# One decode step of attention beside an MLP: wo in four pieces, b1 added by matmuls, heads spread by VectorE

## The chip, the cores and the metric

One NeuronCore of a Trainium2 chip runs the kernel. Its engines are TensorE (PE, with its weight loads as PEld), VectorE (DVE), ScalarE (ACT), GpSimd (POOL) and SyncE (SP), each with an instruction stream of its own; they meet at semaphores. Sixteen DMA engines move data between device memory and the on-chip memory (SBUF). The metric is the device time of one execution in microseconds; lower is better.

## The reference

One token of width 1024 goes through a layer norm. Branch A is attention with 32 query heads over 4 key and value heads, on the last 4096 positions of a cache; branch B is a second layer norm and an MLP of width 3584 with biases b1 and b2. Both are added to the input. All inputs are bf16.

```python
def reference(A_x, A_k_cache, A_v_cache, A_wq, A_wo, B_x, B_w1, B_b1, B_w2, B_b2):
    def _A_ref(x, k_cache, v_cache, wq, wo):
        B, Sq, D = x.shape                      # 1, 1, 1024
        Hq, Dh = 32, 128
        Hkv, Sk = k_cache.shape[1], k_cache.shape[2]   # 4, 65536
        W = min(4096, max(256, Sk // 4))        # 4096
        rep = Hq // Hkv
        q = (lambda x, *d: x.transpose(*d))((x @ wq).reshape(B, Sq, Hq, Dh), 0, 2, 1, 3)
        k = jnp.repeat(k_cache[:, :, Sk - W:, :], rep, axis=1)
        v = jnp.repeat(v_cache[:, :, Sk - W:, :], rep, axis=1)
        scores = jnp.einsum("bhqd,bhkd->bhqk", q, k) * (Dh ** -0.5)
        p = _softmax(scores, axis=-1)
        o = jnp.einsum("bhqk,bhkd->bhqd", p, v)
        return (lambda x, *d: x.transpose(*d))(o, 0, 2, 1, 3).reshape(B, Sq, Hq * Dh) @ wo

    def _B_ref(x, w1, b1, w2, b2):
        y = _layernorm(x, axis=-1)
        h = _gelu(jnp.einsum("bsd,df->bsf", y, w1) + b1)   # 3584 wide
        return jnp.einsum("bsf,fd->bsd", h, w2) + b2

    x = A_x
    xn = _layernorm(x, axis=-1)
    return x + _A_ref(xn, A_k_cache, A_v_cache, A_wq, A_wo) + _B_ref(xn, B_w1, B_b1, B_w2, B_b2)
```

## The kernel before

There is one token, so every matrix is read once and used for one row: about 40 MB come in, 8 MB each for wq and wo, 7 MB each for w1 and w2, and 4 MB each for the keys and the values that are used.

The order is written out by hand, engine by engine. SP issues all large loads on its one queue: the first half of wq, the keys of heads 0 and 1, the second half of wq, the keys of heads 2 and 3, and w1 at once (L234 to L238). Then it waits until DVE has turned the last keys (L311), issues the values over the keys' place and w2 over wq's, waits for the last matmul on w1 (L316) and issues wo in the pieces of WO_CHUNKS (L318 to L321). A piece of n rows gives every one of the 128 partitions n x 2 KB in one run. wo's first 20 rows (TAIL) lie in BIG, the last 12 in KT. ACT issues three small loads on another queue: x, b2, and b1 as 128 runs of 28 values (L170 to L172).

PE's stream, from L423 on, has these stages:

- x is copied to all partitions by two matmuls into banks 0 and 1 (L426); DVE and ACT compute the layer norms from there (L259 to L276). The matmuls of `edge` (L429) set banks 7, 0 and 1 to zero in all rows that matter, with a column HOT that has a single one.
- q: a loop over the two halves of wq, eight matmuls per turn (L443 to L451), into bank 7. Its result is turned by DVE (L293) and copied into the block pattern QBD, five blocks by DVE, three by ACT (L300 to L307). DVE turns keys before and after this (`turn_k`, L283).
- the scores (L459 to L467), in banks 3 to 6, opened by four matmuls with the mask OTHER; DVE takes the maximum (L334), ACT the exponential (L346), DVE turns the result (L350).
- EDGE (L470): two matmuls put x + b2 into bank 7, in which the output is gathered.
- h = y @ w1 in bank 0 (L485 to L488). H8 is its copy, L494 turns it to 128 partitions, DVE adds b1 (L356) and computes the gelu (L361 to L375) into GO, the row of weights of the last loop.
- pv, the values, in bank 1 (L500 to L503); DVE divides and selects (L383) and gathers the heads in ON (L389).
- the last loop, written with branches: `pe_round` (L518) takes four rows of w2 or wo per turn, eight matmuls. After TURN = 4 rounds `pe_turn_o` (L510) breaks in once: four matmuls with E4 spread ON over 128 partitions, and ACT copies the result into GO and OT (L393, L394). 12 rounds in all: 7 for w2, 5 for the first 20 rows of wo.
- the tail, unrolled (L533 to L544): the last 12 rows of wo in pieces of 9, 2 and 1, each row as four small matmuls side by side in four column groups of the array. Then DVE and ACT copy the row out of bank 7 (L397 to L401) and SP stores it.

POOL fills the constants (L177 to L225) and then turns landings into steps of one semaphore, `s_feed`, for which the loops wait (L406 to L421). So a loop's wait is on POOL's step, the tail's waits are on the landings themselves.

Of the kernel before, what the change touches and what calls it, by code (L numbers as in the profile page):

```python
# [9 lines left out]
D = 1024  # L10
# [13 lines left out]
WO_CHUNKS = [8, 12, 9, 2, 1]  # L24
WO_HEAD = 2
# [4 lines left out]
TAIL = 20  # L30
# [5 lines left out]
ROUNDS = 12  # L36
TURN = 4
# [15 lines left out]
def bass_parallel_sum__sliding_block_cached__mixer_channel_mlp__decode_kernel(  # L53
# [19 lines left out]
    def sems(name, n):  # L73
# [13 lines left out]
        "x", "h", "hT", "q", "sc", "pv", "tot", "o2", "fin")}  # L87
    s_feed = nc.alloc_semaphore("S_FEED")

    def sb(name, shape, d):  # L90
        return nc.alloc_sbuf_tensor(name, shape, d)
# [12 lines left out]
    HOT = sb("HOT", [1, 8 + 128], bf16)  # L104
    EDGE = sb("EDGE", [2, 132], bf16)
    XBRP = sb("XBRP", [2, 16 * XP], bf16)
    B1T = sb("B1T", [128, FC], bf16)
# [22 lines left out]
    ON = sb("ON", [32, DH], bf16)  # L130
# [12 lines left out]
    def bank(n, rows=128, first=0):  # L143
        return PS[first:first + rows, n * 512:(n + 1) * 512]
# [6 lines left out]
    def wo_home(row):  # L151
        return (BIG, (FC + row) * D) if row < TAIL else (KT, (row - TAIL) * D)
# [19 lines left out]
    act.dma_start(B1T[:, :], B_b1.rearrange("(p c) -> p c", c=FC)).then_inc(s_b1, 16)  # L172

    def pool_wait():
        pool.wait_ge(POOL.sem, POOL.cnt)
# [3 lines left out]
    POOL.mark(pool.memset(identb[:, :], 0.0))  # L179
    pool_wait()  # L180
# [5 lines left out]
    POOL.mark(pool.memset(HOT[:, :], 0.0))  # L186
    pool_wait()
    C["hot"] = POOL.mark(pool.memset(HOT[:, 7:8], 1.0))
# [3 lines left out]
    POOL.mark(pool.memset(QBD[:, :], 0.0))  # L192
# [33 lines left out]


# [12 lines left out]
    def dve_wait():  # L240
        dve.wait_ge(DVE.sem, DVE.cnt)
# [17 lines left out]
    layernorm_stats(PS[:, 0:1024], 0, "ln1")  # L259
    DVE.mark(dve.tensor_scalar(out=XN[:, :], in0=PS[:, 0:1024], scalar1=MV[:, 0:1], scalar2=SD[:, 0:1],  # L260
# [35 lines left out]
    dve.wait_ge(POOL.sem, C["consts"])  # L296
# [3 lines left out]
    for b in range(4):  # L300
        for c in range(PAIRS):
            to = QD[32 * b:32 * b + 32, c, :, b, 16 * c:16 * c + 16].rearrange("p e (u j) -> p e u j", j=4)
            of = QS[32 * b:32 * b + 32, :, 4 * c:4 * c + 4, :]
            if PAIRS * b + c < 5:
                C["d_QBD"] = DVE.mark(dve.tensor_copy(to, of))  # L305
            else:
                C["a_QBD"] = ACT.mark(act.activation(out=to, in_=of, func=ACTF.Copy))  # L307
# [10 lines left out]
    for j, n in enumerate(WO_CHUNKS):  # L318
        home, first = wo_home(c0)
        sp.dma_start(home[:, first:first + n * D], wo_flat[:, c0 * D:(c0 + n) * D]).then_inc(s_wo[j], 16)  # L320
        c0 += n  # L321

    def spread(first, n):
        return GO[:, LEAD + first * STEP:LEAD + (first + n) * STEP].rearrange(
            "p (r c y) -> p r c y", c=2, y=COPY)[:, :, :, 0:2 * ROUND:2]

    def rows_of(values):
        n = values.shape[1] // ROUND
        return values.rearrange("p (r u) -> p r u", u=ROUND).unsqueeze(2).to_broadcast([128, n, 2, ROUND])
# [12 lines left out]
    for b in range(4):  # L342
# [12 lines left out]
    dve.wait_ge(s_b1, 16)  # L355
    DVE.mark(dve.tensor_tensor(  # L356
        out=HT[:, :].rearrange("p (t c) -> p c t", c=4),
        in0=PS[:, 2 * 512 + 32:2 * 512 + 64].rearrange("p (c t) -> p c t", c=4)[:, :, 0:7],
        in1=B1T[:, :].rearrange("p (t c) -> p c t", c=4), op=ALU.add))
# [18 lines left out]
    DVE.mark(dve.reciprocal(out=REC[:, :], in_=PS[0:64, 2 * 512 + 64:2 * 512 + 65]))  # L378
# [9 lines left out]
    with nc.allow_low_precision(reason="one of the four terms is not zero"):  # L388
        C["on"] = DVE.mark(dve.tensor_reduce(  # L389
            out=ON[:, :], in_=ONM.rearrange("p (g d) -> p d g", g=4), axis=AX.X, op=ALU.add))  # L390
    act.wait_ge(done["o2"], 1)
    o2 = PS[:, 2 * 512:2 * 512 + 32]
    ACT.mark(act.activation(out=spread(FC // ROUND, TAIL // ROUND), in_=rows_of(o2[:, 0:TAIL]), func=ACTF.Copy))  # L393
    C["OT"] = ACT.mark(act.activation(  # L394
        out=OT[:, LEAD:LEAD + 2 * (32 - TAIL):2], in_=o2[:, TAIL:32], func=ACTF.Copy))
# [9 lines left out]

    pool.wait_ge(s_wq[0], 16)  # L406
# [13 lines left out]
    pool.wait_ge(s_wo[WO_HEAD], 16)  # L420
    pool.sem_inc(s_feed, 1)  # L421

    pe.wait_ge(POOL.sem, C["ones"])  # L423
    pe.wait_ge(s_x, 16)
    for i in range(2):
        last = pe.matmul(bank(i), lhsT=onesb[0:1, :], rhs=XB[0:1, 8 * i:8 * i + 8, :])  # L426
    last.then_inc(done["x"], 1)

    def edge(n):  # L429
        pe.matmul(bank(n), lhsT=HOT[:, 8:136], rhs=XB[0:1, 0:8, :], start=True, stop=False, skip_group_check=True)  # L430

    def add(to, lhsT, rhs, **place):
        return pe.matmul(to, lhsT=lhsT, rhs=rhs, start=False, stop=False, skip_group_check=True, **place)  # L433

    turn = pe.alloc_register("turn")
    pe.reg_mov(turn, 1)
    pe.wait_ge(POOL.sem, C["hot"])
    edge(7)
    pe.wait_ge(DVE.sem, C["xz"])
    edge(0)  # L440
    edge(1)
    pe.wait_ge(POOL.sem, C["consts"])
# [9 lines left out]

    pe.wait_ge(ACT.sem, C["q32"])
    for n in range(4):
        pe.matmul(bank(3 + n), lhsT=OTHER[:, :], rhs=ALT[:, :], start=True, stop=False, skip_group_check=True)
    pe.wait_ge(DVE.sem, C["d_QBD"])
    pe.wait_ge(ACT.sem, C["a_QBD"])
    K4 = KT[:, :].rearrange("p (x k) -> p x k", k=128)
    with pe.Fori(0, PAIRS) as c:  # L459
        pe.wait_ge(s_feed, turn)  # L460
        pe.reg_add(turn, turn, 1)
        with pe.Fori(0, 2) as j:
            for n in range(4):
                for u in range(2):
                    last = add(bank(3 + n), QBD[:, bass.ds(c * 512 + j * 256 + u * 128, 128)],
                               K4[:, bass.ds(c * 64 + 16 * n, 16), bass.ds(j * 64 + 32 * u, 32)])
                last.then_inc(done["sc"], 1)  # L467

    pe.wait_ge(s_b2, 16)
    for a in range(2):  # L470
        pe.matmul(bank(7), lhsT=EDGE[:, 1 - a:129 - a], rhs=XB[:, 8 * a:8 * a + 8, :], start=(a == 0), stop=False,
                  skip_group_check=True)
        if a == 0:
            pe.wait_ge(DVE.sem, C["mx"] - 1)

# [3 lines left out]
    first_turn = 1 + len(WQ_CHUNKS) + PAIRS  # L479
    vec, column, limit = (pe.alloc_register(n) for n in ("vec", "column", "limit"))  # L480
    PEO = [pe.engine]
    for register, value in ((vec, 0), (column, 0), (limit, first_turn + TURN)):
        pe.reg_mov(register, value)
# [7 lines left out]
    pe.matmul(PS[0:64, 2 * 512 + 64:2 * 512 + 65], lhsT=B64[:, :], rhs=SUMP[:, :]).then_inc(done["tot"], 1)  # L491
    pe.wait_ge(ACT.sem, C["a_h8"])
    for c in range(4):
        last = pe.matmul(PS[:, 2 * 512 + 32 + 8 * c:2 * 512 + 40 + 8 * c], lhsT=H8[:, c:512:4], rhs=FLIP[:, :])  # L494
# [3 lines left out]
    pe.wait_ge(s_v, 32)  # L498
    V3 = V.rearrange("p (c x) -> p c x", c=PAIRS)
    with pe.Fori(0, 8) as i:  # L500
# [5 lines left out]
    at = type(pe.snap(turn)).of_register_unchecked  # L506
    vec_at, column_at = at(vec, min_val=0, max_val=STEP * (ROUNDS - 1)), at(
        column, min_val=0, max_val=(ROUNDS - 1) * ROUND * D)
    nc.br("pe_round", engines=PEO)
    with nc.body("pe_turn_o", valid_engines=PEO):  # L510
        pe.wait_ge(DVE.sem, C["on"])
        for j in range(4):
            last = pe.matmul(PS[:, 2 * 512:2 * 512 + 32], lhsT=E4[:, j * 128:(j + 1) * 128],
                             rhs=ON[:, j * 32:(j + 1) * 32], start=(j == 0), stop=(j == 3))
        last.then_inc(done["o2"], 1)
        pe.reg_mov(limit, first_turn + ROUNDS)
        nc.br("pe_round", engines=PEO)
    with nc.body("pe_round", valid_engines=PEO):  # L518
        pe.wait_ge(s_feed, turn)
        pe.reg_add(turn, turn, 1)  # L520
        for u in range(ROUND):
            for a in range(2):
                add(bank(7), GO[:, bass.ds(vec_at + (LEAD + 2 * u - ROW - a), 128)],
                    BIG[:, bass.ds(column_at + (u * D + a * 512), 512)])
        pe.reg_add(vec, vec, STEP)
        pe.reg_add(column, column, ROUND * D)
        pe.br_lt(turn, limit, on_true="pe_round", on_false="pe_phase")
    with nc.body("pe_phase", valid_engines=PEO):
        pe.wait_ge(s_feed, turn)
        pe.br_lt(turn, first_turn + ROUNDS, on_true="pe_turn_o", on_false="pe_tail")  # L530
    nc.switch_bb("pe_tail")

    c0 = TAIL  # L533
    for j, n in enumerate(WO_CHUNKS[WO_HEAD:]):
        pe.wait_ge(s_wo[WO_HEAD + j], 16)
        for c in range(c0, c0 + n):
            home, column = wo_home(c)
            rhs = home[:, column:column + D]
            for a in range(4):
                first, column = LEAD + 2 * (c - TAIL) - (0 if a % 2 else ROW), 7 * 512 + a // 2 * 256  # L540
                last = add(PS[32 * a:32 * a + 32, column:column + 256], OT[:, first:first + 32],
                           rhs[:, TAIL_AT[a]:TAIL_AT[a] + 256], tile_position=(0, 32 * a))
        c0 += n
# [31 lines left out]
```

## Time and profile before

| what | value |
|---|---|
| time, median of 3 runs | 99.2 us (99.13 to 99.36) |
| profiled execution, time | 99.2 us |
| its span | 97.55 us |
| bytes read | 39.86 MB, 409 GB/s over the span |
| TensorE clock granted | 1.0 |
| busy: PE, PEld, DVE, ACT, POOL | 73%, 31%, 39%, 8%, 10% of the span |
| last landing of w1, of w2, of wo | 49.33, 76.01, 95.48 us |
| wo issued | 62.16 us |

The span is what the hardware profiler saw of the core; the time is a little longer, since it holds what lies around it. Every time in the text counts from the start of the span. In a row of the timeline the columns are the start, the duration, the engine, the line, the operation, what it writes and reads, and how many of them were joined; the bracket at the end is the idle time ahead of it and what ended it. A row of the DMA queues has the packets, the megabytes and the packets' time as a share of 16 engines in the stretch shown. "Packet records" are the single DMA packets behind these rows, each with its queue, start, duration and size.

### The profile page before, as it was taken

The numbers are of one execution on the slowest core, as the hardware profiler recorded it, in microseconds if no ns is written. First come the engines' busy times: TensorE is split into PE (matmuls) and PEld (weight loads), VectorE is DVE, ScalarE is ACT, GpSimd is POOL, SyncE is SP. The second block draws the span as 40 slices with busy tenths as digits, with TensorE's granted clock in tenths as the row PEclk, the third lists the DMA queues.
The fourth block names the chain that finished last, engine by engine and source line by source line (L and its number), as shares of the span: only waits on it lengthen the run. The fifth ranks groups of instructions, "written<-read, shape, count | busy, mean of one in ns | idle before, by whom it ended". The sixth has DMA issues, their size and how long they took to land.

```text
span 97.6 us, 1259 instructions
## 1 busy us (share of the span) xinstructions
PE 71.6 (73%) x337; PEld 30.1 (31%) x349; DVE 37.9 (39%) x50; ACT 8.1 (8%) x16; POOL 10.2 (10%) x29
## 2 busy tenths in 40 slices
PE   0005000399999973879979999799989999997991
PEld 0001000033444320323334444333344444443450
DVE  0001899899930699950581800050043000000001
ACT  0500000600000023000008000200000010000001
POOL 6999600000000000000000000000000000000000
PEclk9999999999999999999999999999999999999999
DMA  7599999999999998888999999999899998999980
GB/s 215 228 431 444 410 432 437 430 430 443 417 430 464 682 400 376 376 376 376 430 437 430 437 497 443 443 430 400 373 464 423 430 480 363 453 436 416 438 329 1
DMA packets 2229, 39.88 MB, mean 409 GB/s; under 512 B 434, under 2 KB 436, under 8 KB 692
## 3 DMA queue, kind: packets, MB, share of 16 engines
q1 hardware_dynamic: 2020, 39.85, 95.7%
q10 hardware_dynamic: 208, 0.01, 0.1%
q8 instruction: 1, 0.02, 0.1%
HBM read 39.86 MB, written 0.00 MB: 409 GB/s over the span
## 4 chain that ended last, share of the span: by engine, by line
DMA 79%; PE 13%; SPq 4%; issue 1%; DVE 0%
DMA BIG<-in_B_w_dram 47%; DMA KT<-in_A_wo_dram 32%; PE PS L433 13%; SPq L320 2%; SPq L232 1%; SPq L159 1%; DVE Pb L400 0%
## 5 line engine op out<-in xcount | busy, mean ns | idle before, releaser
L433 PE MATMUL PS<-BIG,GO 128*128 x84 | 20.1, 379 | 1.4 <-POOLq L419 0.5
L285 DVE STREAM_TRANSPOSE KT<-KV 128x4096 bf16<-128x4096 bf16 x4 | 17.6, 4432 | 4.8 <-DMA KV<-in_A_k_cache_dram 4.8
L433 PE MATMUL PS<-BIG,XZ 128*128 x64 | 16.2, 418 | 0.0
L433 PEld LDWEIGHTS PS<-BIG,GO 128*128 x96 | 9.3, 98 | 11.8 <-issue 1.7
L433 PE MATMUL PS<-BIG,YZ 128*128 x56 | 12.4, 380 | 0.7 <-DMA BIG<-in_B_w_dram 0.7
L433 PE MATMUL PS<-KT,QBD 128*128 x32 | 8.0, 379 | 2.6 <-DVE QBD L305 1.8
L433 PEld LDWEIGHTS PS<-BIG,XZ 128*128 x64 | 6.7, 105 | 9.9 <-issue 4.5
L400 DVE CAST Pb<-PS 64x256 bf16<-64x256 f32 x1 | 0.4, 417 | 21.7 <-PE PS L433 21.7
L433 PE MATMUL PS<-KV,KT 128*128 x32 | 8.3, 381 | 0.6
L430 PE MATMUL PS<-XBRP,HOT 1*128 1x512 bf16 x3 | 1.7, 620 | 9.0 <-DVE XZ L275 9.0
L433 PEld LDWEIGHTS PS<-BIG,YZ 128*128 x56 | 5.4, 96 | 7.5 <-issue 1.9
L426 PE MATMUL PS<-XBRP,onesb 1*128 1x512 bf16 x2 | 1.0, 605 | 8.2 <-DMA XBRP<-in_A_x_dram 8.2
L433 PEld LDWEIGHTS PS<-KT,QBD 128*128 x32 | 3.1, 96 | 7.5 <-issue 5.4
L245 DVE BATCH_NORM_STATS2 BN<-PS 128x6 f32<-128x512 f32 x2 | 1.3, 689 | 9.3 <-PE PS L426 9.3
L433 PEld LDWEIGHTS PS<-KV,KT 128*128 x32 | 3.1, 96 | 5.4 <-issue 3.9
L334 DVE TENSOR_REDUCE MX<-PS 128x1 f32<-128x1024 f32 x2 | 2.4, 1220 | 4.4 <-PE PS L433 4.4
L383 DVE SCALAR_TENSOR_TENSOR QBD<-PS,REC,HALF 32x256 f32<-32x256 f32 x2 | 0.9, 473 | 7.0 <-PE PS L433 6.9
L430 PEld LDWEIGHTS PS<-XBRP,HOT 1*128 1x128 bf16 x3 | 0.3, 118 | 10.2 <-DVE XZ L275 9.9
L350 DVE STREAM_TRANSPOSE KT<-Pb 128x2048 bf16<-128x2048 bf16 x1 | 2.3, 2312 | 2.1 <-ACT Pb L346 2.1
L356 DVE TENSOR_TENSOR HT<-PS,B1T 128x28 f32<-128x28 f32 x1 | 0.2, 209 | 7.4 <-PE PS L494 7.4
L346 ACT ACTIVATE Pb<-PS,NMB 128x2048 bf16<-128x2048 f32 x1 | 2.0, 1967 | 13.0 <-DVE NMB L343 13.0
L426 PEld LDWEIGHTS PS<-XBRP,onesb 1*128 1x128 bf16 x2 | 0.1, 98 | 8.2 <-issue 8.2
(76 smaller groups left out, 37.6 us busy)
## 6 DMA issues: line engine op xcount, KB each, us to landing
BIG<-in_A_wq_dram SPq DMA_DIRECT2D x2, 4096.0 KB, 18.9
BIG<-in_B_w_dram SPq DMA_DIRECT2D x1, 7168.0 KB, 46.0
KV<-in_A_k_cache_dram SPq DMA_DIRECT2D x2, 2048.0 KB, 23.2
KV<-in_A_v_cache_dram SPq DMA_DIRECT2D x2, 2048.0 KB, 13.4
BIG<-in_B_w_dram SPq DMA_DIRECT2D x1, 4096.0 KB, 24.6
BIG<-in_B_w_dram SPq DMA_DIRECT2D x1, 3072.0 KB, 31.2
BIG<-in_A_wo_dram SPq DMA_DIRECT2D x1, 3072.0 KB, 25.6
KT<-in_A_wo_dram SPq DMA_DIRECT2D x1, 2304.0 KB, 30.6
```

The costliest lines, as they stand in the source:

```text
L159: sp.dma_start(dst[:, c0 * width:(c0 + n) * width].rearrange("p (c n) -> p c n", c=n), src[:, c0:c0 + n, :],).then_inc(semaphores[j], 16)
L232: sp.dma_start(KV[:, c * 8192:(c + 1) * 8192], pairs(A_k_cache, c)).then_inc(s_k[c], 16)
L245: DVE.mark(dve.bn_stats(out=BN[:, 12 * n + 6 * i:12 * n + 6 * i + 6], in_=src[:, 512 * i:512 * i + 512]))
L285: C["kt", n] = DVE.mark(dve.transpose(KT[:, n * 4096:(n + 1) * 4096], KV[:, n * 4096:(n + 1) * 4096]))
L320: sp.dma_start(home[:, first:first + n * D], wo_flat[:, c0 * D:(c0 + n) * D]).then_inc(s_wo[j], 16)
L334: C["mx"] = DVE.mark(dve.tensor_reduce(out=MX2[:, n:n + 1], in_=S[:, 1024 * n:1024 * n + 1024], axis=AX.X, op=ALU.max))
L346: C["exp"] = ACT.mark(act.activation(out=Pb[:, :], in_=S, func=ACTF.Exp, bias=NMB[:, 0:1], scale=SCALE, accum_out=SUMP[:, 0:1]))
L350: C["d_pt"] = DVE.mark(dve.transpose(PT[:, 0:2048], Pb[:, :]))
L383: DVE.mark(dve.scalar_tensor_tensor(out=ONM.rearrange("p (i c d) -> p i c d", i=2, c=PAIRS)[:, i], in0=PS[rows, 512:1024].rearrange("p (c ...
L426: last = pe.matmul(bank(i), lhsT=onesb[0:1, :], rhs=XB[0:1, 8 * i:8 * i + 8, :])
L430: pe.matmul(bank(n), lhsT=HOT[:, 8:136], rhs=XB[0:1, 0:8, :], start=True, stop=False, skip_group_check=True)
L433: return pe.matmul(to, lhsT=lhsT, rhs=rhs, start=False, stop=False, skip_group_check=True, **place)
```

## The change

- wo comes in pieces of 16, 11, 4 and 1 rows instead of 8, 12, 9, 2 and 1, all into BIG. The last loop takes the first 16 rows (11 rounds in all), the unrolled tail the last 16. POOL's last step now follows the first piece of wo.
- b1 comes as 32 runs of 112 values. Four matmuls with E4, placed after the q loop, put it into the place in bank 2 (`turned`) on which the turned h is then added; DVE copies the sum instead of adding b1. The wait for the values stands among the matmuls that turn h.
- DVE spreads the heads: ON is turned as float32, then in four pieces into O2. The four matmuls on ON and the break in the last loop go, and this loop becomes a plain counted one.
- The banks are opened by ACT, which copies zeros from QBD into banks 0, 1 and 7; the three `edge` matmuls and HOT go. x is copied into banks 2 and 3. POOL zeroes QBD earlier, and steps `s_feed` only after its constants are done.
- EDGE's two matmuls move from after the scores to before them; of the eight blocks of QBD DVE copies four, ACT four, and PE's wait for ACT's part moves into the loop.

The changed lines, with "..." between them:

```diff
...
-WO_CHUNKS = [8, 12, 9, 2, 1]
-WO_HEAD = 2
+WO_CHUNKS = [16, 11, 4, 1]
+WO_HEAD = 1
...
-TAIL = 20
+TAIL = 16
...
-ROUNDS = 12
-TURN = 4
+ROUNDS = 11
...
-        "x", "h", "hT", "q", "sc", "pv", "tot", "o2", "fin")}
+        "x", "h", "hT", "q", "sc", "pv", "tot", "fin")}
...
-    HOT = sb("HOT", [1, 8 + 128], bf16)
...
-    B1T = sb("B1T", [128, FC], bf16)
+    B1R = sb("B1R", [32, F // 32], bf16)
...
-    ON = sb("ON", [32, DH], bf16)
+    ON = sb("ON", [32, DH], f32)
+    ONT = sb("ONT", [32, DH], f32)
+    O2 = sb("O2", [128, 32], f32)
...
-    def wo_home(row):
-        return (BIG, (FC + row) * D) if row < TAIL else (KT, (row - TAIL) * D)
...
-    act.dma_start(B1T[:, :], B_b1.rearrange("(p c) -> p c", c=FC)).then_inc(s_b1, 16)
+    act.dma_start(B1R[:, :], B_b1.rearrange("(p c) -> p c", p=32)).then_inc(s_b1, 16)
...
+    C["QBD"] = POOL.mark(pool.memset(QBD[:, :], 0.0))
...
-    POOL.mark(pool.memset(HOT[:, :], 0.0))
-    pool_wait()
-    C["hot"] = POOL.mark(pool.memset(HOT[:, 7:8], 1.0))
...
-    POOL.mark(pool.memset(QBD[:, :], 0.0))
...
+    act.wait_ge(POOL.sem, C["QBD"])
+    ACT.mark(act.activation(out=PS[:, 0:1024], in_=QBD[:, :], func=ACTF.Copy))
+    ACT.mark(act.activation(out=bank(7), in_=QBD[:, 0:512], func=ACTF.Copy))
+
...
-    layernorm_stats(PS[:, 0:1024], 0, "ln1")
-    DVE.mark(dve.tensor_scalar(out=XN[:, :], in0=PS[:, 0:1024], scalar1=MV[:, 0:1], scalar2=SD[:, 0:1],
+    layernorm_stats(PS[:, 1024:2048], 0, "ln1")
+    DVE.mark(dve.tensor_scalar(out=XN[:, :], in0=PS[:, 1024:2048], scalar1=MV[:, 0:1], scalar2=SD[:, 0:1],
...
-    dve.wait_ge(POOL.sem, C["consts"])
...
-            if PAIRS * b + c < 5:
+            if PAIRS * b + c < 4:
...
-        home, first = wo_home(c0)
-        sp.dma_start(home[:, first:first + n * D], wo_flat[:, c0 * D:(c0 + n) * D]).then_inc(s_wo[j], 16)
+        first = (FC + c0) * D
+        sp.dma_start(BIG[:, first:first + n * D], wo_flat[:, c0 * D:(c0 + n) * D]).then_inc(s_wo[j], 16)
...
-    dve.wait_ge(s_b1, 16)
-    DVE.mark(dve.tensor_tensor(
-        out=HT[:, :].rearrange("p (t c) -> p c t", c=4),
-        in0=PS[:, 2 * 512 + 32:2 * 512 + 64].rearrange("p (c t) -> p c t", c=4)[:, :, 0:7],
-        in1=B1T[:, :].rearrange("p (t c) -> p c t", c=4), op=ALU.add))
+    DVE.mark(dve.tensor_copy(
+        HT[:, :].rearrange("p (t c) -> p c t", c=4),
+        PS[:, 2 * 512 + 32:2 * 512 + 64].rearrange("p (c t) -> p c t", c=4)[:, :, 0:7]))
...
-    DVE.mark(dve.reciprocal(out=REC[:, :], in_=PS[0:64, 2 * 512 + 64:2 * 512 + 65]))
+    DVE.mark(dve.reciprocal(out=REC[:, :], in_=PS[0:64, 3 * 512:3 * 512 + 1]))
...
-    with nc.allow_low_precision(reason="one of the four terms is not zero"):
-        C["on"] = DVE.mark(dve.tensor_reduce(
-            out=ON[:, :], in_=ONM.rearrange("p (g d) -> p d g", g=4), axis=AX.X, op=ALU.add))
-    act.wait_ge(done["o2"], 1)
-    o2 = PS[:, 2 * 512:2 * 512 + 32]
-    ACT.mark(act.activation(out=spread(FC // ROUND, TAIL // ROUND), in_=rows_of(o2[:, 0:TAIL]), func=ACTF.Copy))
+    DVE.mark(dve.tensor_reduce(
+        out=ON[:, :], in_=ONM.rearrange("p (g d) -> p d g", g=4), axis=AX.X, op=ALU.add))
+    dve_wait()
+    DVE.mark(dve.transpose(ONT[:, :], ON[:, :]))
+    dve_wait()
+    for n in range(4):
+        C["o2"] = DVE.mark(dve.transpose(
+            O2[32 * n:32 * n + 32, :], ONT[:, :].rearrange("p (q h) -> p h q", q=4)[:, 8 * n:8 * n + 8, :]))
+    act.wait_ge(DVE.sem, C["o2"])
+    ACT.mark(act.activation(out=spread(FC // ROUND, TAIL // ROUND), in_=rows_of(O2[:, 0:TAIL]), func=ACTF.Copy))
...
-        out=OT[:, LEAD:LEAD + 2 * (32 - TAIL):2], in_=o2[:, TAIL:32], func=ACTF.Copy))
+        out=OT[:, LEAD:LEAD + 2 * (32 - TAIL):2], in_=O2[:, TAIL:32], func=ACTF.Copy))
...
+    pool_wait()
...
-    pool.wait_ge(s_wo[WO_HEAD], 16)
-    pool.sem_inc(s_feed, 1)
-
...
+    turn = pe.alloc_register("turn")
+    pe.reg_mov(turn, 1)
...
-        last = pe.matmul(bank(i), lhsT=onesb[0:1, :], rhs=XB[0:1, 8 * i:8 * i + 8, :])
+        last = pe.matmul(bank(2 + i), lhsT=onesb[0:1, :], rhs=XB[0:1, 8 * i:8 * i + 8, :])
...
-    def edge(n):
-        pe.matmul(bank(n), lhsT=HOT[:, 8:136], rhs=XB[0:1, 0:8, :], start=True, stop=False, skip_group_check=True)
-
...
-    turn = pe.alloc_register("turn")
-    pe.reg_mov(turn, 1)
-    pe.wait_ge(POOL.sem, C["hot"])
-    edge(7)
...
-    edge(0)
-    edge(1)
-    pe.wait_ge(POOL.sem, C["consts"])
...
+    pe.wait_ge(s_b1, 16)
+    turned = PS[:, 2 * 512 + 32:2 * 512 + 64].rearrange("p (c t) -> p c t", c=4)[:, :, 0:7]
+    for q in range(4):
+        pe.matmul(turned, lhsT=E4[:, q * 128:(q + 1) * 128],
+                  rhs=B1R[:, q * FC:(q + 1) * FC].rearrange("p (t c) -> p c t", c=4),
+                  start=(q == 0), stop=False, skip_group_check=True)
+        if q == 0:
+            pe.wait_ge(s_b2, 16)
+
...
+    for a in range(2):
+        pe.matmul(bank(7), lhsT=EDGE[:, 1 - a:129 - a], rhs=XB[:, 8 * a:8 * a + 8, :], start=(a == 0), stop=False,
+                  skip_group_check=True)
...
-    pe.wait_ge(ACT.sem, C["a_QBD"])
...
+        pe.wait_ge(ACT.sem, C["a_QBD"])
...
-    pe.wait_ge(s_b2, 16)
-    for a in range(2):
-        pe.matmul(bank(7), lhsT=EDGE[:, 1 - a:129 - a], rhs=XB[:, 8 * a:8 * a + 8, :], start=(a == 0), stop=False,
-                  skip_group_check=True)
-        if a == 0:
-            pe.wait_ge(DVE.sem, C["mx"] - 1)
-
...
-    first_turn = 1 + len(WQ_CHUNKS) + PAIRS
-    vec, column, limit = (pe.alloc_register(n) for n in ("vec", "column", "limit"))
-    PEO = [pe.engine]
-    for register, value in ((vec, 0), (column, 0), (limit, first_turn + TURN)):
-        pe.reg_mov(register, value)
...
-    pe.matmul(PS[0:64, 2 * 512 + 64:2 * 512 + 65], lhsT=B64[:, :], rhs=SUMP[:, :]).then_inc(done["tot"], 1)
+    pe.matmul(PS[0:64, 3 * 512:3 * 512 + 1], lhsT=B64[:, :], rhs=SUMP[:, :]).then_inc(done["tot"], 1)
...
-        last = pe.matmul(PS[:, 2 * 512 + 32 + 8 * c:2 * 512 + 40 + 8 * c], lhsT=H8[:, c:512:4], rhs=FLIP[:, :])
+        last = add(turned[:, c], H8[:, c:512:4], FLIP[:, 0:7])
+        if c == 0:
+            pe.wait_ge(s_v, 32)
...
-    pe.wait_ge(s_v, 32)
...
-    at = type(pe.snap(turn)).of_register_unchecked
-    vec_at, column_at = at(vec, min_val=0, max_val=STEP * (ROUNDS - 1)), at(
-        column, min_val=0, max_val=(ROUNDS - 1) * ROUND * D)
-    nc.br("pe_round", engines=PEO)
-    with nc.body("pe_turn_o", valid_engines=PEO):
-        pe.wait_ge(DVE.sem, C["on"])
-        for j in range(4):
-            last = pe.matmul(PS[:, 2 * 512:2 * 512 + 32], lhsT=E4[:, j * 128:(j + 1) * 128],
-                             rhs=ON[:, j * 32:(j + 1) * 32], start=(j == 0), stop=(j == 3))
-        last.then_inc(done["o2"], 1)
-        pe.reg_mov(limit, first_turn + ROUNDS)
-        nc.br("pe_round", engines=PEO)
-    with nc.body("pe_round", valid_engines=PEO):
+    with pe.Fori(0, ROUNDS) as t:
...
-                add(bank(7), GO[:, bass.ds(vec_at + (LEAD + 2 * u - ROW - a), 128)],
-                    BIG[:, bass.ds(column_at + (u * D + a * 512), 512)])
-        pe.reg_add(vec, vec, STEP)
-        pe.reg_add(column, column, ROUND * D)
-        pe.br_lt(turn, limit, on_true="pe_round", on_false="pe_phase")
-    with nc.body("pe_phase", valid_engines=PEO):
-        pe.wait_ge(s_feed, turn)
-        pe.br_lt(turn, first_turn + ROUNDS, on_true="pe_turn_o", on_false="pe_tail")
-    nc.switch_bb("pe_tail")
+                add(bank(7), GO[:, bass.ds(t * STEP + (LEAD + 2 * u - ROW - a), 128)],
+                    BIG[:, bass.ds(t * (ROUND * D) + (u * D + a * 512), 512)])
...
-            home, column = wo_home(c)
-            rhs = home[:, column:column + D]
+            rhs = BIG[:, (FC + c) * D:(FC + c + 1) * D]
```

## The prediction

> **What bounds the kernel now.** I read the table of DMA queues first, then the chain that ended last, then the DMA queues again in short windows, then the timeline of the end.
>
> ```profile
> q1 hardware_dynamic: 2020, 39.85, 95.7%
> q10 hardware_dynamic: 208, 0.01, 0.1%
> q8 instruction: 1, 0.02, 0.1%
> ```
>
> SP's queue q1 keeps the 16 DMA engines busy for 95.7% of the span. The packet records say the same more sharply: the first data packet starts at 1.84 us, the last ends at 95.18 us, and no engine has a hole between them.
>
> ```profile
> 3.30 46.02 DMA BIG<-in_B_w_dram
> 49.33 0.35 issue
> 49.68 12.46 PE PS L433 x56
> ...
> 63.95 31.52 DMA KT<-in_A_wo_dram
> 95.48 0.04 issue
> 95.52 0.32 PE PS L433 x4
> 95.84 0.02 issue
> 95.87 0.42 DVE Pb L400
> ```
>
> The chain names PE for 12.46 us in its middle, but this is not a bound: wo is issued at 62.16 when the w2 rows that end at 76.01 are still queued ahead of it. The reader is to see the end: the last row of wo lands at 95.48, four matmuls, two copies and the store follow, and the span ends at 97.55. So an edit counts only if it changes how much engine time the stream needs, makes the stream wait, or lets PE be late when the last row lands.
>
> One line of the first table matters more than its 0.1%. The queues from 94.92 to 95.95 us:
>
> ```profile
> q8 instruction: 1, 0.02, 5.6%
> q1 hardware_dynamic: 16, 0.01, 4.1%
> ```
>
> From 93.90 to 94.92 there is no q8. A packet of 16,384 bytes of instructions starts at 94.93 (packet records) and takes 5.6% of 16 engines in 1.03 us, that is 0.92 us (record: 0.931; data packets of that size take 0.612). It follows directly on the last semaphore write (94.922) that its engine owes to wo, so it costs nothing today. The 16 engines write that last semaphore between 94.655 and 95.175; this one is 0.25 us ahead of the last.
>
> ```profile
> 93.81 0.89 PEld L433 LDWEIGHTS PS<-KT,GO 128*32 128x32 bf16 x36 [0.61 <-DMA KT<-in_A_wo_dram]
> ...
> 94.89 0.12 PEld L433 LDWEIGHTS PS<-KT,GO 128*32 128x32 bf16 x8 [0.19 <-DMA KT<-in_A_wo_dram]
> 95.52 0.10 PEld L433 LDWEIGHTS PS<-KT,GO 128*32 128x32 bf16 x4 [0.51 <-DMA KT<-in_A_wo_dram]
> ```
>
> PE enters its unrolled tail at 93.81. POOL executes its last instruction at 93.63 (the increment at L421). These are the only engines that come to a new place in their code in the 1.3 us before the packet; DVE, ACT and SP stand in waits until 95.86 or later.
>
> **The change part by part.**
>
> *The stream.* Bytes are the same. A packet carries a row or chunk of one partition, 8 packets per engine for 128 partitions. wo before: 612 + 912 + 686 + 159 + 84 ns (16, 24, 18, 4, 2 KB) = 2453. After: 1213 (32 KB) + 837 (22 KB, between 686 and 912) + 310 (8 KB, between 159 and 612) + 84 = 2444. 9 ns x 8 packets = 0.07 us less, and one semaphore write (0.009) less. b1 goes from 128 packets of 56 bytes (11 ns, 8 per engine) to 32 of 224 bytes (about 16 ns, between 13 at 128 bytes and 52 at 1 KB; 2 per engine): 88 - 32 = 0.06 us less. Sum -0.13 us; bounds 0 and -0.2.
>
> *The start.* POOL zeroes QBD 0.94 us earlier in its list, drops HOT (0.3 us); zeros for XZ come at about 3.8 instead of 2.8, needed at 18.35. ACT opens banks: one copy of 1024 (between 0.60 for 512 and 1.97 for 2048, take 1.1), one of 512 (0.6), and the built program holds one table load more (1.28). From 2.8 us this ends near 7; ACT's next work is at 11.04. Without that cover L252 would be up to 1.3 us late, then the q matmuls; they end at 35.86, and DVE needs their result only after turning K until 36.85, so 1.0 us of it would still be hidden. PE drops three edge matmuls (0.62 each), two of them at 18.64 just ahead of q, which may start 1 us sooner; nothing waits for that. If PE's slow first matmuls (0.43 us apart until 23.8, 0.22 after) are only moved into q, q starts 0.96 earlier and ends no later than now.
>
> *The middle.* Four b1 matmuls (nearest: L494, four in 0.29 us) and the two EDGE matmuls (0.91) now stand between q and the scores, where PE idles 1.76 us for QBD; cover gone, they'd cost 0.3 to 1.2 us of a path with room until w1 lands at 49.33. They leave the place at 48.09, so PE is ready for h earlier and waits for the same landing. The waits for b1 and b2 there meet landings at 16.65 and 10.52. One QBD copy goes from DVE (0.18) to ACT (0.3); turn 3 of K ends 0.18 us sooner, v is issued sooner, behind w1 in the queue: nothing. The added wait for v ahead of the h turning meets a landing at 59.04, PE gets there at 62.8.
>
> *Heads.* DVE: five transposes replace four PE matmuls. Bounds for each: 0.15 (smallest DVE instruction) to 0.67 (L293), so 0.75 to 3.4 us after 74.12; I take 1.3 (small tiles lie near the low row). ACT's two copies (0.4) end before 78, PE needs them for the first wo round, after wo's first chunk lands near 85.7: 8 us of cover.
>
> *The last rounds.* PE runs 56 w2 matmuls from 72.24 at 0.216 us each to 84.3. wo's first 16 rows land at 80.86 + 8 x 0.606 (the pace from 80.86 to 88.13 for 12 rows) - 0.1 = 85.6. PE took 0.2 us from landing to matmul at 88.13, so 32 matmuls run from 85.85 to 92.75. Eleven rows landed at 92.3; tail rows go at 0.109 us each (36 matmuls in 0.98 us), until 94.0. Four rows land at 94.73 and take 0.48, until 95.2; the last row would land at 95.35. PE is in time, with 0.15 to 0.7 us to spare. An h-like pace (12.45/56 = 0.222) costs 0.2 of this.
>
> *The instruction packet.* What triggers it comes earlier. If PE's way into the tail does it: PE gets there near 92.8 instead of 93.81. The built programs, branch labels left out, hold 192 PE instructions ahead of the tail before and 180 after, so a fixed place in the code lies 12 instructions (0.16 us at 8 per 0.109 us) deeper in the tail. Net 0.85 us earlier: 94.93 becomes about 94.1. If POOL's last instruction does it: that now follows the 16 rows, 85.7, and the packet falls near 87. Either way its engine then still has wo packets to move (without it, it would end at 94.93 - 0.13 = 94.80). Does a late packet of another queue wait behind q1? From 1.80 to 6.02 us and from 6.02 to 6.50:
>
> ```profile
> q1 hardware_dynamic: 48, 1.57, 102.5%
> ...
> q1 hardware_dynamic: 15, 0.49, 236.9%
> q10 hardware_dynamic: 15, 0.00, 2.5%
> ```
>
> x, issued at 0.81, is let in after three q1 packets per engine, in the middle of a chunk of eight; it does not wait for the stream to empty. So the packet is pushed in and its engine ends 0.931 later: 95.73, against 95.05 for the last of the others. The last landing goes from 95.48 - 0.13 = 95.35 to 96.03, 0.68 later. Bounds: on an engine that ends first, 0.931 - 0.52 = 0.41; on the last one, 0.93; not in the stream at all, 0.
>
> The Trainium skill says in "DMA: Bandwidth & Descriptors", section "Queues, rings and completion order", that an engine takes turns between the queues that have work, packet by packet; by that rule, too, the fetch would cut into the stream, and the rows of x agree. "Runtime: NRT & Kernel Launch", section "Instruction fetch mechanics", has code fetched in 16 KiB blocks by the sequencer's own DMA queue, which the 16,384 bytes here bear out, and calls crossing a block "mostly hidden"; by that the sum would stay at -0.13 (the second case below).
>
> Sum: -0.13 + 0.68 = +0.55 us. The profiled execution has a span of 97.55 and a time of 99.2, 1.65 outside; 99.2 is also the median of the three runs. 99.2 + 0.55 = 99.75.
>
> **The rivals.** *The fetch stays hidden* (25 in 100): it comes behind what its engine has queued, or is not asked for earlier. For it: today's packet starts exactly when its engine has nothing left, which a queue behind everything would also give. Against it: x. Then 99.2 - 0.13 = 99.07: not slower, at most a hair faster. It decides if the packet starts after its engine's last wo packet (94.8).
>
> *PE becomes late at the end* (6 in 100). The pv loop takes 8.3/32 = 0.26 to 0.275 us per matmul at four per turn. At 0.275 the 32 matmuls end at 94.65, 11 rows at 95.85, five more at 96.4, against a start of the last four at 95.52 now: +0.9 with the last row's own time, 100.1. It decides above (93.5 - 85.85)/32 = 0.24 per matmul. Against it: h and q, eight per turn like the new loop, show 0.222.
>
> *The engine of the packet ends early in this run* (7 in 100): +0.41 - 0.13 gives 99.5.
>
> **How the numbers follow.** Forecast 62, hidden 25, PE late 6, early engine 7. Predicted 99.75; its own range is 99.5 to 100.0 (0.41 to 0.93 of push, 0 to -0.2 of saving). The range for 8 in 10 reaches down to the hidden case: 99.0 to 100.0. About 0.2% (0.2 us) is what a measurement of this kernel can tell from no change. Below 99.0 lies the hidden case with a saving at its bound: 12. Within: most of the hidden case, part of the early engine: 20. Slower: 68.
>
> **What would show it.** In the page after: q8's packet in a window before 94.8; one of the last semaphores some 0.7 us behind the others; the last landing near 96.0; PE waiting over 1 us before its last four matmuls. Right but mis-sized: the packet early, the last landing off by the engine's place. Wrong: q8 after 94.8 and the end at 97.4; or PE's rounds ending after 93.5. A hole in the DMA rows near 43 or 62, or q matmuls later than 36.9, would refute the covers of the middle.

## The result, and the profile after

The median went from 99.22 us (99.10 to 99.54) to 98.91 us (98.78 to 99.42), 22 runs of each on one chip: a ratio of 0.9975 [0.9965, 0.9986], 0.31 us faster. The forecast was 99.75 and slower.

The profiled span did not move: 97.55 before, 97.56 after. Each run also lists its span to 0.1 us. After, the mean span is 97.52; before, it is 97.60 to 97.70 in the five sessions of the experiments below. So about 0.1 us comes from inside the span. What a run takes beyond its span has a median of 1.62 to 1.66 us before and 1.41 after, and this is the larger part of the gain, 0.2 us.

The DMA queues of the changed kernel over the span, then (second fence) from 94.94 to 95.95 us; packets, megabytes, share of 16 engines:

```profile
q1 hardware_dynamic: 1876, 39.85, 95.4%
q10 hardware_dynamic: 112, 0.01, 0.1%
q8 instruction: 1, 0.02, 0.1%
```

```profile
q8 instruction: 1, 0.02, 5.8%
q1 hardware_dynamic: 11, 0.01, 3.4%
```

q1 has 144 packets fewer and q10 96 fewer, as the diff says. The instruction packet, forecast at 94.1, is where it was: its record starts at 94.947, 6 ns after the start of its engine's last semaphore write (before, 94.928 after 94.922). It costs nothing.

The chain that ended last (start, duration):

```profile
63.09 31.76 DMA BIG<-in_A_wo_dram
94.86 0.04 issue
94.90 0.94 PE PS L430 x20
95.84 0.02 issue
95.87 0.42 DVE Pb L400
```

It now goes over the piece of four rows, which lands at 94.86, and joins the 20 matmuls that follow into one stretch, since the ends of matmuls are modelled. The timeline of PE's weight loads shows more of the last rounds and the tail:

```profile
86.06 1.41 PEld L430 LDWEIGHTS PS<-BIG,GO 128*128 x8 [1.65 <-issue]
87.87 1.41 PEld L430 LDWEIGHTS PS<-BIG,GO 128*128 x8 [0.41 <-issue]
89.73 1.41 PEld L430 LDWEIGHTS PS<-BIG,GO 128*128 x8 [0.45 <-issue]
91.54 1.41 PEld L430 LDWEIGHTS PS<-BIG,GO 128*128 x8 [0.40 <-issue]
93.38 1.10 PEld L430 LDWEIGHTS PS<-BIG,GO 128*32 128x32 bf16 x44 [0.42 <-issue]
94.90 0.34 PEld L430 LDWEIGHTS PS<-BIG,GO 128*32 128x32 bf16 x16 [0.42 <-DMA BIG<-in_A_wo_dram]
95.52 0.10 PEld L430 LDWEIGHTS PS<-BIG,GO 128*32 128x32 bf16 x4 [0.28 <-DMA BIG<-in_A_wo_dram]
```

The last line shows that PE still waits: it is idle for 0.28 us until the last row has landed at 95.48 (0.51 us before), and its last four weight loads start at 95.52, as before. So the last landing still sets the end. Four turns of eight matmuls take (93.38 - 86.06)/4 = 1.83 us each, 0.229 per matmul: the counted loop leaves some 0.4 us between the weight loads of two turns. So PE enters the tail at 93.38, where 92.8 was forecast (93.81 before). The heads, in DVE's timeline, are turned first as a whole, then in four pieces:

```profile
74.15 0.30 DVE L387 STREAM_TRANSPOSE ONT<-ON 32x128 f32<-32x128 f32 x1
74.48 0.98 DVE L390 STREAM_TRANSPOSE O<-ONT 32x32 f32<-32x32 f32 x4
```

The five turnings take 0.30 + 0.98 = 1.28 us; 1.3 was forecast.

### The profile page after: what moved, and what is told of

Read it like the earlier page. It is cut to its first block, busy times and chain, and to the rows that moved or that the text cites. A ratio compares the mean times of both kernels' runs of the same rounds, so it can differ in the third digit from the quotient of the medians.

```text
span 97.6 us, 1274 instructions
## 1 busy us (share of the span) xinstructions
PE 71.6 (73%) x343; PEld 30.1 (31%) x354; DVE 39.0 (40%) x54; ACT 11.2 (11%) x20; POOL 9.9 (10%) x27
## 4 chain that ended last, share of the span: by engine, by line
DMA 80%; PE 14%; SPq 3%; issue 1%; DVE 0%
DMA BIG<-in_B_w_dram 47%; DMA BIG<-in_A_wo_dram 33%; PE PS L430 14%; SPq L231 1%; SPq L157 1%; SPq L318 1%; DVE Pb L400 0%
## 5 line engine op out<-in xcount | busy, mean ns | idle before, releaser
L430 PE MATMUL PS<-BIG,XZ 128*128 x64 | 16.9, 433 | 10.2 <-DVE B L277 10.2
L430 PE MATMUL PS<-BIG,GO 128*128 (+1 forms) x141 | 21.9, 332 | 2.0 <-POOLq L420 1.2
L430 PEld LDWEIGHTS PS<-BIG,GO 128*128 (+1 forms) x152 | 10.1, 97 | 14.1 <-issue 6.4
L430 PE MATMUL PS<-KT,QBD 128*128 x32 | 8.9, 436 | 0.8 <-ACT QBD L305 0.8
L290 ACT ACTIVATE Pb<-PS 128x512 bf16<-128x512 f32 x1 | 0.6, 597 | 16.9 <-PE PS L430 16.9
```

## The experiments

All ratios are to the kernel before on the same chip, with 95% intervals. "Outside" is the median over a kernel's runs of time less span, which is listed to 0.1 us. Lengths of PE's and DVE's instruction streams are counted in the built programs, without labels: DVE has 57 instructions before and 59 after; PE has 192 ahead of the tail before and 180 after. Added matmuls write 32 x 2 values to a place in bank 4 that the scores overwrite; added waits are for semaphores that have long been reached.

### The parts of the change

`r2_wo` is the kernel before with the new pieces of wo; `r3_b1` the kernel before with b1 as 32 runs and four matmuls; `r4_rest` the changed kernel with old wo and old b1.

```diff
-WO_CHUNKS = [8, 12, 9, 2, 1]
-TAIL = 20
-ROUNDS = 12
+WO_CHUNKS = [16, 11, 4, 1]
+TAIL = 16
+ROUNDS = 11
```

```diff
-    B1T = sb("B1T", [128, FC], bf16)
+    B1R = sb("B1R", [32, F // 32], bf16)
...
+    for q in range(4):
+        pe.matmul(turned, lhsT=E4[:, q * 128:(q + 1) * 128],
+                  rhs=B1R[:, q * FC:(q + 1) * FC].rearrange("p (t c) -> p c t", c=4),
+                  start=(q == 0), stop=False, skip_group_check=True)
```

> The kernel before with wo in 16, 11, 4 and 1 rows, all in BIG; nothing else is changed. Theory S (the gain is engine time of the stream, as the packet sums have it): 0.08 us faster, 99.14. Theory G (the gain of 0.31 lies mostly outside the stream's sums): 99.2, with the gain in the kernel that has the rest of the change.

> The kernel before with b1 in 32 runs, added by matmuls; nothing else is changed. Theory S: 0.06 us faster, 99.16. Theory G: 99.2. If b1's 96 packets fewer are worth more than their own 11 ns, because each is squeezed between two data packets of its engine: 99.0.

> The changed kernel with wo in 8, 12, 9, 2, 1 rows and b1 in 128 runs as before; the heads, the banks, EDGE and the plain loop stay changed. Theory S: 99.2, no gain. Theory G: 98.9 to 99.05, most of the gain.

| kernel | time, us | ratio | mean span | outside |
|---|---|---|---|---|
| r2_wo | 99.30 | 0.9999 [0.9986, 1.0013] | 97.58 | 1.76 |
| r3_b1 | 100.75 | 1.0150 [1.0130, 1.0171] | 99.16 | 1.64 |
| r4_rest | 99.56 | 1.0026 [1.0013, 1.0040] | 98.04 | 1.55 |

No part alone is faster. Inside its span r2_wo gains 0.12 us on the kernel before, which has 97.70 on the same chip; its 1.76 outside takes the gain away. r3_b1 is the surprise: its instruction packet starts at 86.81, in the stream, and its last landing is at 97.13, 1.2 us after the other 15 engines' 95.93. But r3_b1 and r4_rest also differ in another way: B1T and B1R have different sizes, and what lies behind them in SBUF (BIG among it) moves to addresses 32 bytes off a multiple of 64. `e5_b1_old` (old b1) and `e6_wo_old` (old wo) undo one part with a gap that keeps the later places as they were (e6: the same modulo 512 bytes); `e7_shift32` is the changed kernel with only such a shift.

```diff
+    sb("GAP", [128, 16], bf16)
```

> The changed kernel with b1 in 128 runs, added by DVE, as before; a gap of 160 bytes keeps BIG, KT and KV at their places in SBUF. Theory S (b1 is worth the engine time of its packets): 0.06 us slower than the changed kernel, 98.97. Theory O (most of the 0.31 us lies outside the span, 1.42 instead of 1.63 us, and belongs to b1's part): 99.1 to 99.2, with the time outside the span back near 1.6.

> The changed kernel with wo in 8, 12, 9, 2, 1 rows, all in BIG, with a gap that keeps the places of BIG, KT and KV the same modulo 512 bytes. Theory S: 0.08 us slower than the changed kernel, 98.99. Theory O with wo's part as the one outside the span: 99.1 to 99.2.

> The changed kernel with a gap of 32 bytes ahead of KV, so that KV, KT and BIG, where all large loads end, begin 32 bytes off a multiple of 64; nothing else is changed. Theory D (the packets of the two kernels with part of the change, r3 and r4, were longer by up to 12 ns because their targets lay 32 bytes off): 0.4 to 0.5 us slower than the changed kernel, 99.35, with packets of 2 KB at 84 to 96 ns instead of 84. Theory C (their slower stream came from the code, not from the places): 98.91.

| kernel | time, us | ratio | mean span | outside |
|---|---|---|---|---|
| e5_b1_old | 99.07 | 0.9979 [0.9968, 0.9990] | 97.55 | 1.56 |
| e6_wo_old | 98.98 | 0.9973 [0.9959, 0.9986] | 97.62 | 1.40 |
| e7_shift32 | 99.39 | 1.0010 [1.0001, 1.0019] | 97.97 | 1.42 |

The shift alone costs 99.39 - 98.91 = 0.48 us, nearly all of it inside the span. Its packets are longer: those of 2 KB take 84 to 93 ns instead of 84 (most still 84), those of 22 KB 842 in the mean instead of 836, those of 24 KB 916 instead of 912. r4_rest has such longer packets too, and nearly the same mean span, so it measured mostly this. With places kept, old b1 costs 0.16 us, nearly all of it outside the span (1.56 against 1.41, to which the last group of experiments comes back), and old wo 0.07. The mean span grows by 0.03 and 0.10, against 0.06 and 0.07 forecast; these are too small to be told from each other.

### The instruction packet

Does the fetch follow PE's place in its code, and what does it cost in mid-stream? `r1_pad`, `e9_twenty` and `e12_twelve` are the changed kernel with 123, 10 and 6 added matmuls, two instructions each, ahead of q; `e8_eight` is the kernel before with 4, behind q.

```diff
+    for _ in range(4):
+        pe.matmul(PS[0:32, 4 * 512:4 * 512 + 2], lhsT=onesb[0:1, 0:32], rhs=onesb[0:1, 0:2])
```

> The changed kernel with 123 tiny matmuls (246 instructions) added ahead of the wait for xz, where PE idles from 9.2 to 18.6 us, so that PE reaches any fixed place of its code 246 instructions sooner and its stream is longer by them. Theory A (a fetch of instructions cuts into the stream wherever it falls, and the forecast failed only because it stayed at the end): a second q8 packet between 9 and 25 us, its engine 0.93 us behind, the last landing 0.4 to 0.9 us later, time 99.3 to 99.8. Theory B (a fetch is served only when its engine has no data left to move): no q8 packet before 94.6, time 98.9, or later by far if PE runs out of code.

> The kernel before with four tiny matmuls (eight instructions) ahead of the wait for q32, where PE idles; as many instructions as r3 has there, nothing else is changed. Theory A (r3 was slow because its PE code is eight instructions longer ahead of the last loop, so that the fetch came at 86.8 us, in the middle of the stream): q8 near 87 us, one engine about 1.2 us behind, time 100.2 to 100.5. Theory C (r3 was slow through b1's new layout): q8 at 94.9, time 99.2.

> The changed kernel with ten tiny matmuls (twenty instructions) ahead of the wait for xz, where PE idles; PE's code ahead of the tail is then 200 instructions, as in the two kernels whose fetch came at 86.8. Theory A (a fixed place of the code asks for the fetch; with 200 it lies ahead of the tail): q8 before 90 us, one engine 1.2 to 1.5 us behind, time 100.1 to 100.4. Theory E (the fetch belongs to the entry into the tail, whatever stands ahead): q8 at 94.9, time 98.9.

> The same with six tiny matmuls (twelve instructions): 192 ahead of the tail, as in the kernel before. Theory A: the place lies a few instructions into the tail, q8 near 94.9, time 98.9 to 99.0. Theory E: the same. If the place has a margin of fewer than twelve instructions here: 100.1 to 100.4.

| kernel | PE ahead of the tail | packet starts, us | last landing (others' last) | time, us | ratio |
|---|---|---|---|---|---|
| after | 180 | 94.95 | 95.48 | 98.91 | 0.9975 |
| e12_twelve | 192 | 94.85 | 95.36 | 98.94 | 0.9973 [0.9959, 0.9988] |
| e8_eight | 200 | 86.86 | 96.92 (95.50) | 100.58 | 1.0157 [1.0112, 1.0202] |
| e9_twenty | 200 | 76.54 | 96.56 (95.34) | 101.00 | 1.0151 [1.0109, 1.0193] |
| r1_pad | 426 | 15.12 and 95.15 | 96.88 (95.42) | 100.11 | 1.0086 [1.0062, 1.0109] |

So PE's count of instructions moves the packet, and POOL's end does not: in the changed kernel POOL is done at 85.8 and the packet stays. 192 ahead of the tail are still safe in both kernels; at 200 the packet falls into the stream, as it did in r3_b1 (200 too). Why 200 bring it to 76.54 in one kernel and to 86.86 in the other is not shown. e8_eight's queues from 86.8 to 87.8 us:

```profile
q1 hardware_dynamic: 31, 0.36, 88.1%
q8 instruction: 1, 0.02, 5.8%
```

The packet takes its 0.93 us among 24 KB packets of wo. The data packet that starts as it ends takes 1411 ns instead of 912 (1115 instead of 611 in r1_pad, 1712 instead of 1213 in e9_twenty), so the engine loses 0.93 + 0.50 = 1.43 us. The end of e8_eight's chain:

```profile
63.95 32.97 DMA KT<-in_A_wo_dram
96.92 0.04 issue
96.96 0.32 PE PS L433 x4
97.28 0.02 issue
97.31 0.42 DVE Pb L400
```

The reader is to see the last landing at 96.92, where it stood at 95.48 before, with nothing else between it and the end: 1.44 us later. One packet on one of 16 engines has become the kernel's time, 100.58 - 99.24 = 1.34 us on this chip. (One of the six runs took 101.99; it widens the interval.)

e9_twenty loses more, and not to the packet alone. Its runs fall into two groups: 100.00 and 100.05 with a span of 98.6, and four of 100.94 to 101.23 with 99.5 to 99.8. The profile is of a long one. There the first piece of wo lands at 86.86, because the engine of the packet ends 1.24 us behind the others (85.62), and PE stands still until then:

```profile
87.15 0.50 PEld L430 LDWEIGHTS PS<-BIG,GO 128*128 x3 [2.50 <-issue]
87.92 0.15 PEld L430 LDWEIGHTS PS<-BIG,GO 128*128 x1 [0.27 <-issue]
...
95.86 1.65 PEld L430 LDWEIGHTS PS<-BIG,GO 128*32 128x32 bf16 x64 [0.42 <-issue]
```

After 2.50 us without work PE's granted clock is 0.57 to 0.58 from 87 to 91 us, where it is 1.00 in the changed kernel, and its next matmuls stand 0.43 us apart until 90.8. PE comes to the tail at 95.86 and runs all 64 matmuls of it in one go, past the last landing at 96.56: here PE is late, and the span ends 0.9 us after what the landing alone would give (97.55 - 95.48 = 2.07 us before, 99.53 - 96.56 = 2.97 here). Shorter waits, 2.30 us in e8_eight and 1.72 in r1_pad, were followed by a clock of 1.00. That the other three long runs have the same cause is not shown.

r1_pad also shows that a requested packet waits. PE runs the added matmuls from 9.12, for 3.44 us:

```profile
9.12 3.44 PE L433 MATMUL PS<-onesb 1*32 1x2 bf16 x123
```

It then waits until 18.3, yet the packet starts at 15.115, at least 15.12 - 12.56 = 2.6 us after the last instruction of PE that could have asked for it. In between its engine has moved four 16 KB packets, and it moves four more of the same chunk behind it.

### The time outside the span

`e10_dve1` is the changed kernel with one more DVE instruction (60). `e11_dve2`, `f1_dve58`, `f2_dve60` and `f3_dve65` are the kernel before with 2, 1, 3 and 8 more; `f4_act25` the kernel before with two more on ACT. Two waits build into one instruction. `g1_58` and `g2_57` are the changed kernel with one and two DVE instructions fewer: g1 waits for pv in the place of tot, and g2 also joins the wait for the zeros to an earlier instruction.

```diff
+    dve.wait_ge(s_x, 16)
+    dve.wait_ge(s_b2, 16)
```

```diff
-    dve.wait_ge(done["tot"], 1)
+    dve.wait_ge(done["pv"], 8)
...
-    dve.wait_ge(done["pv"], 8)
```

> The changed kernel with one more wait on DVE, for b1, which has long landed: the one instruction that DVE has more in the kernel with b1 in the old form (e5). Theory B (the time outside the span follows b1's layout): 98.91, 1.41 us outside. Theory I (it follows the number of instructions of an engine's stream): 99.05, 1.55 us outside.

> The kernel before with two more instructions on DVE (four waits for loads that have long landed): 59, as in the changed kernel. Theory I: the time outside the span falls from 1.63 to about 1.41 us, time 99.0. Theory B: 1.63 outside, 99.2.

> The kernel before with one more instruction on DVE (two waits for loads that have long landed): 58. Theory I1 (outside the span, time falls with the length of DVE's stream): between 1.64 and 1.41 us outside. Theory I2 (it jumps with the place where the stream ends): either 1.41 or 1.64, nothing between.

> The kernel before with three more instructions on DVE: 60, as in e5, e10 and r4. If DVE's count alone sets the time outside the span: 1.50 to 1.55 us, time 99.05 to 99.1. If e5, e10 and r4 had it from something else: 1.41, time 98.95.

> The kernel before with eight more instructions on DVE: 65. Theory I1: 1.4 us outside or less. Theory I2: any of 1.41 to 1.76, by the place.

> The kernel before with two more instructions on ACT (25 instead of 23) and none on DVE. If it is DVE's stream alone: 1.64 us outside, 99.2. If any engine's stream does it: another value than 1.64.

> The changed kernel with one instruction less on DVE: the wait for tot goes, since the wait for pv, which PE reaches later, takes its place. DVE's stream is 58 long, as in f1. Theory I2 (the number of DVE's instructions sets the time outside the span, by the place where the stream ends, in any kernel): 1.26 us outside, time 98.75, faster than the kernel before and the changed one. If f1's 1.26 came from where its added wait stands: 1.41, time 98.91.

> The changed kernel with two instructions less on DVE: the same, and the wait for the zeros joins an instruction that waits for nothing else. DVE's stream is 57 long, as in the kernel before. Theory I2: 1.64 us outside, time 99.1, so that what is left of the change is its 0.1 us inside the span. If the rest of the change is worth more outside: 98.9 to 99.0.

| kernel | DVE instructions | time, us | ratio | mean span | outside |
|---|---|---|---|---|---|
| before | 57 | 99.22 | 1 | 97.60 to 97.70 | 1.62 to 1.66 |
| f4_act25 | 57 | 99.25 | 1.0000 [0.9987, 1.0013] | 97.66 | 1.66 |
| f1_dve58 | 58 | 98.87 | 0.9960 [0.9945, 0.9975] | 97.60 | 1.26 |
| e11_dve2 | 59 | 98.95 | 0.9977 [0.9967, 0.9987] | 97.59 | 1.41 |
| f2_dve60 | 60 | 99.06 | 0.9979 [0.9966, 0.9991] | 97.53 | 1.52 |
| f3_dve65 | 65 | 99.44 | 1.0021 [1.0009, 1.0033] | 98.23 | 1.25 |
| g2_57 | 57 | 99.23 | 0.9996 [0.9984, 1.0007] | 97.55 | 1.66 |
| g1_58 | 58 | 98.80 | 0.9948 [0.9929, 0.9968] | 97.52 | 1.30 |
| after | 59 | 98.91 | 0.9975 [0.9965, 0.9986] | 97.52 | 1.41 |
| e10_dve1 | 60 | 99.00 | 0.9975 [0.9964, 0.9986] | 97.46 | 1.50 |

The same count gives the same time outside in both kernels, to 0.04 us in this table (e5_b1_old and r4_rest, 60 each, have 1.56 and 1.55), and two more on ACT change nothing. r2_wo does not fit: 1.76 at 57. e11_dve2 has the whole gain of the change with none of its work; g2_57 has all of its work, and no gain that can be told from none. g1_58 has the lowest median of all, though its interval still touches that of the changed kernel.

Why DVE's count does this is not shown. The trace holds one trail: packets of 8,192 bytes of instructions on another queue, q14. In the kernels with up to 59 they all lie ahead of the span's work; in the four with 60 (e10_dve1, f2_dve60, e5_b1_old, r4_rest) one starts at 98.8 to 99.5, after the span's end; in f3_dve65 one falls into the stream. Its queues from 75.8 to 76.3 us:

```profile
q1 hardware_dynamic: 13, 0.21, 106.0%
q14 instruction: 1, 0.01, 3.9%
```

The last landing of f3_dve65 is 95.98 against 95.58 on the other engines: the mean span is 0.6 us longer than before, and 0.4 less outside offsets most of it. r2_wo's 1.76 has no explanation in these runs; r3_b1 has 1.64 at 56.

## Why the prediction was wrong

**The stream, -0.13 us: right within what can be measured.** The packets have the forecast sizes and durations: 836 ns for 22 KB (837), 309 for 8 KB (310), 16 for a run of b1 (16). Mean spans are 0.1 us shorter. Its two terms, 0.07 and 0.06, are too small to be shown one by one.

**The covers: right.** ACT's opening of the banks ends at 6.94 ("near 7") and its next work is still at 11.04. The q matmuls end at 36.3, 0.5 later than "no later than now", within the 1.0 us of cover; the last turning of K starts at 38.46, as before. The heads' 1.28 us are covered.

**The last rounds: in time, but slower than said.** Landings were forecast at 85.6, 92.3, 94.73 and 95.35, and came at 85.76, 92.40, 94.86 and 95.48. The pace was 0.229 per matmul, not 0.216 (nor the 0.222 named as a risk). PE still waited 0.42 us for the four rows and 0.28 for the last, inside the forecast 0.15 to 0.7. The rival of a late PE (above 0.24) stayed short of its condition; in e9_twenty PE was late, by a lower clock.

**The instruction packet, +0.68 us: this step failed.** It reads "Net 0.85 us earlier: 94.93 becomes about 94.1. ... Either way its engine then still has wo packets to move". The packet started at 94.95, not 94.1, behind the wo packets, and cost nothing. The trigger was named rightly (PE's place in its code), and what a fetch does in mid-stream was too, though undersized: 0.93 was taken, 1.43 us of the engine's time are measured. What failed is the time of the start. PE came to the tail only 0.43 us earlier, not 1.0. And a requested packet does not come at once: in r1_pad it takes at least 2.6 us. Nor is the delay a fixed one, as the forecast took it to be: from PE's way into the tail to the packet it is 94.93 - 93.81 = 1.12 us before and 94.95 - 93.38 = 1.57 after. Where in the code the request is made is not shown. In 14 of the 16 kernels whose q8 packet comes in the tail alone, its record starts exactly 6 ns after the start of a last semaphore write, the step at which packets of one engine follow each other; in the other two (r4_rest, f3_dve65) 18 and 31 ns after the end of one. So many hits, at times from 94.74 to 95.19, point to a queue: the engine seems to hold wo's last packets already and to move them first. That it holds them is inferred, not shown. The row that was read against this, x let in after three packets, does not refute it: x was issued at 0.81 and came after 6.02, a delay longer than the 0.85 us at stake. The rival "the fetch stays hidden" was the case, with a chance of 25 in 100.

The Trainium skill, "Runtime: NRT & Kernel Launch", section "Instruction fetch mechanics", calls the crossing of a block "mostly hidden". That holds for the changed kernel, and not for e8_eight, e9_twenty, r1_pad and r3_b1, where the last landing comes 1.2 to 1.5 us behind that of the other engines. The Trainium skill's "DMA: Bandwidth & Descriptors", section "Queues, rings and completion order", has an engine change queues at the ends of packets, which it counts at some 9 to 17 descriptors. The trace agrees that queues with work take turns, but after single records: in r1_pad two runs of b1 stand one by one between 32 KB packets (11.44 and 12.66 us). By that rule a fetch cuts in as soon as it is queued; it does not tell how long the queueing takes, and this was the missing number.

**A term that was missing, -0.2 us.** The sum took 1.65 us outside the span as fixed. It fell to 1.41, and e11_dve2 and g2_57 show that it goes with DVE's count, with or without the rest of the change. The hidden case was priced at 99.2 - 0.13 = 99.07; with the missing term, 99.07 - 0.23 = 98.84, against 98.91 measured. Without this term the change would lie within what a measurement can tell from none, as g2_57 does (0.9996).

## What to carry to other kernels

In a kernel bound by its DMA stream, count every engine's instructions as transfers too: eight instructions more on PE, which do next to nothing, cost 1.3 us. Before a small gain is credited to an edit, run the old kernel with the new instruction counts and the same buffer places, since both move the time by more than the edit may. Read time less span as a term of its own.

## What the runs showed of the hardware

- A data packet that follows a fetch of 16,384 bytes on its engine took 0.50 us more at three sizes (611, 912 and 1213 ns alone).
- After 2.50 us without work PE's granted clock was 0.57 for some 4 us (e9_twenty); after 2.30 (e8_eight) it was 1.00.
- Buffers 32 bytes off a multiple of 64 cost 0.48 us of a 95 us stream (e7_shift32).
- DVE's instruction count changes the time outside the span: 1.66, 1.26, 1.41, 1.52 and 1.25 us at 57, 58, 59, 60 and 65. What decides it stays open.
